# Channel attention and a highway layer on one core: held output stores, one chunk of v moved from DMA to TensorE, and a freer order of the t and x matmuls

## The chip, the core and the metric

The kernel runs on one core of a Trainium2 chip. The metric is the device time of one execution in microseconds (us). Five runs of the kernel before gave 279.01, 279.09, 278.99, 278.85 and 279.81, so the median is 279.01.

The core has a matrix engine (TensorE, PE in the profile, with its weight loads as PEld), a vector engine (VectorE, DVE), a scalar engine (ScalarE, ACT), GpSimd (POOL) and SyncE (SP). In this kernel POOL issues the loads and SP issues the stores and the DMA transposes. [...]

## The reference

There are four batches of q, k and v, each 6336 x 256 in f32. What is computed for each batch, cut to what matters:

```python
qn = q / (norm(q, axis=1) + 1e-6)            # norms over the 6336 rows
kn = k / (norm(k, axis=1) + 1e-6)
a = softmax(kn.T @ qn / tau)                 # 256 x 256, rows sum to 1
x = v @ a                                    # 6336 x 256
H = maximum(x @ w_h, 0)
T = 1 / (1 + exp(-(x @ w_t + b_t)))
out = T * H + (1 - T) * x
```

The attention is among the 256 channels, so all rows of q and k of a batch must have been read before the first output row of that batch.

## The kernel before

**Tiling.** A batch's rows are 48 steps of 128 rows, grouped into six chunks of eight steps, and a tail of 192 rows that counts as two steps. A chunk of q, k or v is one load of 1.05 MB that casts f32 to f16 on the way.

**Stage 1** (`stage1`, L381) takes a step of q and k and adds six matmuls into two PSUM banks, `sg0` and `sg1`: k'q, and k'k and q'q for the norms. There are 50 steps in a batch, 200 in all.

**The chain** (`plan_chain`, L409) follows the last step of a batch. It takes the diagonals from PSUM on DVE, powers on POOL, a broadcast matmul (`cqb`), scaling, exp, transposes (`eps`), the products of a with the two weights (`ah`), and leaves `mr`: 3 x 256 columns, which give x, h and t from v directly.

**Stage 2** (`plan_stage2`, L782) works on pairs of steps. There are 25 pairs in a batch, 100 in all, counted by g from 0 to 99. v is needed transposed. In batches 0 to 2, PE transposes it into PSUM (`transposes`, `vtps`) and ACT or DVE copies it out (`evac_vt`, `vtsb`). In batch 3, SP's DMA transposes it, a chunk at a time (`transpose_chunk`, L614, into `vT`). For each pair PE then makes h, t and x (4 matmuls each; x is accumulated onto `d`). ACT makes d from h (`relu`) and the gate from t. DVE makes `pp` and then `o`. Before t, its bank is filled with the bias: by a copy on ACT or DVE, or, from g = 66 on for every second pair, by a row matmul (`row0`, L673) into `sg1`, which stage 1 no longer needs.

**Order of the work.** The kernel is laid out by a planner, `Plan.run`, before anything is issued. It is a list scheduler: each task has an engine, a key, a length, things it waits for, and buffers it takes and gives back. An engine that is free takes the ready task with the lowest key. The order that comes out is the program's order. DMAs of POOL and SP are taken in order of their keys. `slot_of` (L355) spreads the steps of stage 1 of batches 1 to 3 between the pairs of stage 2: `ENDS` says at which pair stage 1 of a batch should end, `HEAD` how many steps come before the first pair.

**Buffers.** Nine chunks of q, nine of k, seven of v, three of the output `o`, four of `vT`, five of `vtsb`. A load waits for the buffer that it takes over. The rules that the change touches most are these:

```python
h = plan.add("PE", g, 0.435, 0.64, [ev] + ready[b] + ends_of[h_bank], ...)
t = plan.add("PE", g + 0.1, ..., [h] + b_ld + own + before + ends_of[t_bank], ...)
x = plan.add("PE", g + 0.2, 0.43, 0.63, [r, t], ...)
```

So t comes after h of its pair, and x after t and after relu. A store goes out as soon as its chunk is done (key g + 2). The identity and other constants are made first on POOL, then come the loads of batch 0: chunks 0 to 4, tail, chunk 5 in halves (both halves of q, then both of k).

## Time and profile before

| what | before |
|---|---|
| median of five runs | 279.01 us |
| the profiled execution's own time | 279.23 us |
| its span | 277.5 us |
| PE busy | 254.6 us (92%), 2610 matmuls |
| DVE, ACT, POOL busy | 181.4, 175.0, 54.5 us |
| loads (queue of POOL) | 39.20 MB written, 71.4% of 16 engines' span |
| stores and transposes (queue of SP) | 29.20 MB, 31.4% |
| HBM read and written | 78.38 and 25.95 MB |
| first and last start of PE's matmuls | 9.12 and near 271.6 us |

The span is the time from the first to the last instruction in the profile; the rest of an execution's time lies around it. Busy time of PE is a sum over matmuls that overlap, so it says where PE is at work, not how fast. The timeline gives the start of each instruction, its length, and in brackets how long the engine was idle before it and what ended that. A wait for several things is put down to the one that came last.

### The profile page before, as it was taken

The numbers are of one execution on the slowest core, as the hardware profiler recorded it, in microseconds if no ns is written. First come the engines' busy times: TensorE is split into PE (matmuls) and PEld (weight loads), VectorE is DVE, ScalarE is ACT, GpSimd is POOL, SyncE is SP. The second block draws the span as 40 slices with busy tenths as digits, with TensorE's granted clock in tenths as the row PEclk, the third lists the DMA queues.
The fourth block names the chain that finished last, engine by engine and source line by source line (L and its number), as shares of the span: only waits on it lengthen the run. The fifth ranks groups of instructions, "written<-read, shape, count | busy, mean of one in ns | idle before, by whom it ended". The sixth has DMA issues, their size and how long they took to land.

```text
span 277.5 us, 6499 instructions
## 1 busy us (share of the span) xinstructions
PE 254.6 (92%) x2610; PEld 228.0 (82%) x2610; DVE 181.4 (65%) x366; ACT 175.0 (63%) x328; POOL 54.5 (20%) x104
## 2 busy tenths in 40 slices
PE   0696879999999999999999999999999888999992
PEld 0595877899999898999999888999999767888881
DVE  1000035576766886777776886777777887898994
ACT  1000016666767776777767766777767779898982
POOL 7221445220212240211112421111111300000000
PEclk9998999999999999999999999999999999999997
DMA  6999999999999999999999999999999999999984
GB/s 110 210 215 213 210 207 212 216 213 288 257 246 282 287 212 288 240 272 279 244 262 287 257 243 280 220 296 264 242 284 289 234 261 171 355 222 313 251 307 180
DMA packets 29581, 68.80 MB, mean 248 GB/s; under 512 B 14832, under 2 KB 16496, under 8 KB 26608
## 3 DMA queue, kind: packets, MB, share of 16 engines
q0 software_dynamic: 12608, 39.20, 71.4%
q1 hardware_dynamic: 16944, 29.20, 31.4%
q8 instruction: 20, 0.33, 0.5%
q14 instruction: 9, 0.07, 0.1%
HBM read 78.38 MB, written 25.95 MB: 376 GB/s over the span
## 4 chain that ended last, share of the span: by engine, by line
PE 64%; DMA 30%; POOL 2%; DVE 2%; issue 1%; ACT 0%; DVEq 0%; POOLq 0%; ACTq 0%
PE t L642 12%; PE d L642 12%; PE h L642 12%; PE sg L393 10%; DMA v<-in_v_dram 10%; DMA k<-in_k_dram 8%; DMA vT<-v 7%; DMA q<-in_q_dram 6%; PE sg L394 5%; PE sg L395 5%; PE vtps L612 4%; PE t L673 1%; DVE pp L703 1%; POOL q L286 1%; PE ah L551 1%
## 5 line engine op out<-in xcount | busy, mean ns | idle before, releaser
L393 PE MATMUL sg<-q,k 128*128 128x256 f16 x384 | 96.0, 281 | 13.7 <-DMA k<-in_k_dram 13.7
L642 PEld LDWEIGHTS <-vtsb 128*128 128x128 f16 (+1 forms) x900 | 83.4, 99 | 9.8 <-issue 1.9
L394 PE MATMUL sg<-k 128*128 128x128 f16 x384 | 86.3, 225 | 0.0
L395 PE MATMUL sg<-q 128*128 128x128 f16 x384 | 85.6, 223 | 0.0
L703 DVE SCALAR_TENSOR_TENSOR pp<-uu,d 128x512 f32<-128x512 f32 (+1 forms) x100 | 68.3, 684 | 17.3 <-PE d L642 12.1
L696 ACT ACTIVATE uu<-t 128x512 f32<-128x512 f32 (+1 forms) x100 | 59.6, 597 | 27.4 <-PE t L642 25.4
L682 ACT ACTIVATE d<-h 128x512 f32<-128x512 f32 (+1 forms) x100 | 58.4, 584 | 22.3 <-PE h L642 22.0
L722 DVE SCALAR_TENSOR_TENSOR o<-h,pp 128x512 f32<-128x512 f32 x96 | 66.1, 689 | 2.9
L393 PEld LDWEIGHTS <-k 128*128 128x128 f16 x384 | 38.4, 100 | 16.1 <-DMA k<-in_k_dram 14.5
L405 ACT COPY t<-bias_all 128x512 f32<-128x512 f32 (+1 forms) x78 | 46.0, 589 | 1.9
L642 PE MATMUL d<-mr,vtsb 128*128 128x256 f16 x300 | 44.8, 272 | 0.1
L642 PE MATMUL t<-mr,vtsb 128*128 128x256 f16 x300 | 44.8, 272 | 0.1
L642 PE MATMUL h<-mr,vtsb 128*128 128x256 f16 x300 | 44.8, 272 | 0.0
L407 DVE COPY vtsb<-vtps 128x256 f32<-128x256 f32 (+1 forms) x62 | 26.1, 420 | 26.2 <-PE vtps L612 25.9
L395 PEld LDWEIGHTS <-q 128*128 128x128 f16 x384 | 38.6, 101 | 5.4
L394 PEld LDWEIGHTS <-k 128*128 128x128 f16 x384 | 38.6, 101 | 1.9
L642 PEld LDWEIGHTS <-vT 128*128 128x128 f16 x288 | 28.1, 98 | 5.7 <-DMA vT<-v 1.1
L612 PE MATMUL vtps<-ident,v 128*128 128x128 f32 x144 | 27.7, 274 | 1.8 <-ACT vtsb L405 1.1
L441 DVE SCALAR_TENSOR_TENSOR junk<-sg,ident 128x128 f32<-128x128 f32 x16 | 4.6, 287 | 37.3 <-PE sg L395 36.7
L484 ACT COPY gs<-sg 128x256 f32<-128x256 f32 x8 | 2.6, 376 | 38.2 <-DVE junk L441 38.2
L286 POOL DMA_DIRECT2D v<-in_v_dram x24 | 13.0, 543 | 48.7 <-PE d L642 9.5
L286 POOL DMA_DIRECT2D k<-in_k_dram x25 | 13.4, 538 | 39.9 <-DMA k<-in_k_dram 16.6
(66 smaller groups left out, 176.9 us busy)
## 6 DMA issues: line engine op xcount, KB each, us to landing
out_dram<-o SPq DMA_DIRECT2D x23, 1024.0 KB, 9.1
v<-in_v_dram POOLq DMA_DIRECT2D x24, 512.0 KB, 20.5
q<-in_q_dram POOLq DMA_DIRECT2D x23, 512.0 KB, 21.4
k<-in_k_dram POOLq DMA_DIRECT2D x23, 512.0 KB, 20.5
out_dram<-o SPq DMA_DIRECT2D x2, 512.0 KB, 2.6
out_dram<-ot SPq DMA_DIRECT2D x4, 192.0 KB, 6.6
q<-in_q_dram POOLq DMA_DIRECT2D x2, 256.0 KB, 14.7
k<-in_k_dram POOLq DMA_DIRECT2D x2, 256.0 KB, 12.0
```

What stands on the lines that cost most here:

```text
L286: nc.gpsimd.dma_start(out=t[:, s : s + n, :], in_=main_rows(src)[:, j * CH + s : j * CH + s + n, :])
L393: nc.tensor.matmul(sg[c][:, 0:C], kc, qa, start=first, stop=False)
L394: nc.tensor.matmul(sg[c][:, C : C + P], kc, kc, start=False, stop=False)
L395: nc.tensor.matmul(sg[c][:, C + P : C + 2 * P], qa[:, cs], qa[:, cs], start=False, stop=last)
L405: nc.scalar.copy(out=out, in_=in_)
L407: nc.vector.tensor_copy(out=out, in_=in_)
L612: nc.tensor.transpose(ps[:, u, 0:nr], words, ident0[0:nr, 0:nr])
L642: nc.tensor.matmul(out[0:nr, u, :], vt[u][kt][:, 0:nr], mr[kt][:, col * C : (col + 1) * C], **flags(u, kt))
L682: nc.scalar.activation(out=d[0:nr, :, :], in_=ps_t["h", b, i][0:nr, :, :], func=Act.Relu, scale=0.5)
L696: nc.scalar.activation(out=uu[0:nr, :, :], in_=ps_t.pop(("t", b, i))[0:nr, :, :], func=Act.Tanh, scale=-0.5)
L703: nc.vector.scalar_tensor_tensor(out=pp[0:nr, :, :], in0=el.pop(("uu", b, i))[0:nr, :, :], scalar=1.0, in1=ps_t.pop(("d", b, i))[0:nr, :, ...
L722: nc.vector.scalar_tensor_tensor(out=ot, in0=ps_t.pop(("h", b, i))[0:nr, :, :], scalar=0.0, in1=el.pop(("pp", b, i))[0:nr, :, :], op0=AluO ...
```

## The change

It has these parts.

1. **Held stores.** There are seven output buffers in place of three. `plan_holds` moves each chunk's store behind a small DMA on SP (`hold`, 1 KB) that reads the first row of the chunk four later, and so waits for the first result of that chunk. From pair 63 on nothing is held; the stores still held then go out together.
2. **Loads.** q, k and v have five buffers each. The constants come behind the first q and k on POOL (`serial`). Chunk 5 of batch 0 comes in quarters, q and k in turn, and stage 1 of batch 0 takes the tail before it. v of a chunk is loaded three pairs later in rank instead of two or ten earlier.
3. **First v chunk of batch 3.** It is transposed by PE, in f16, four transposes for a pair, and copied out by ACT or DVE; the other five chunks and the tail still go by DMA, planned 12 pairs ahead instead of 8, with three `vT` buffers instead of four.
4. **t and x.** t no longer waits for h. x waits for relu and only follows t on PE (`follows`: placed after t, without a wait for t's result in the plan).
5. **Keys.** `PRIO` gives each kind of task its own offset before and after pair 65; `ENDS` becomes 14.5, 35.5, 68; `HEAD` 7; nine `vtsb` buffers instead of five.

The code for sums of squares off PE (`APART`) is switched off, since `APART` is 0. The diff, cut:

```diff
-QK_BUFS = 9
-V_BUFS = 7
-AHEAD = 8
-MOVE = 100e3
-LOOK = 1.6
-POW = 1.0
-HEAD = 8
+QK_BUFS = 5
+V_BUFS = 5
+O_BUFS = 7
+LAG = 4
+UNTIL = 63
+AHEAD = 12
+BY_DMA = 1
+MOVE = 150e3
+APART = 0
+V_AHEAD = -3
+
+PRIO = {
+    "tr": (-1.66, -2.13), "ev": (-1.74, 0.56), "h": (1.61, 1.23), "bias": (1.7, -2.32),
+    "t": (2.04, 1.45), "relu": (-0.66, 0.47), "x": (1.97, 2.65), "gate": (-0.06, 5.26),
+    "prod": (0.43, -3.06), "res": (3.19, -3.22), "s1": (-0.71, 1.24), "sq": (-1.37, 0.36),
+}
+POW = 0.75
+HEAD = 7
-ENDS = [18, 42, 66]
+ENDS = [14.5, 35.5, 68]
...
-            x.n, x.left, x.at = n, len(x.deps), 0.0
+            x.n, x.left, x.at = n, len(x.deps) + len(x.follows), 0.0
...
                 free[e] = t + x.pitch
+                release(followers.get(x, ()), free[e])
...
-        "vT": 4, "vT_t": 1, "o": 3, "ot": 1, "uu": 3, "pp": 3, "vtsb": 5, "mr0": 2, "mr1": 2,
+        "sq": 2, "vT": 3, "vT_t": 1, "o": O_BUFS, "ot": 1, "uu": 3, "pp": 3, "vtsb": 9, "mr0": 2, "mr1": 2,
...
     consts = plan.add("POOL", len(plan.tasks), 0.6, 1.5, [], constants)
+    consts.serial = True
...
-    plan_load("q", 0, NJ - 1, 2)
-    plan_load("k", 0, NJ - 1, 2)
+    for part in range(4):
+        plan_load("q", 0, NJ - 1, 4, part)
+        plan_load("k", 0, NJ - 1, 4, part)
...
-                seq.append((NP * b + CH // 2 * j - (10 if b == B - 1 else 2), 1, "v", b, j))
+                seq.append((NP * b + CH // 2 * j - V_AHEAD, 1, "v", b, j))
...
+    def by_dma(b, j):
+
+        return natural(b) and j >= BY_DMA
+
+    def order_of(b):
+
+
+        if b:
+            return list(range(NS))
+        return [*range(S - CH), *range(S, NS), *range(S - CH, S)]
...
-            words = sub("v", b, 2 * i + u).bitcast(f32)
-            nc.tensor.transpose(ps[:, u, 0:nr], words, ident0[0:nr, 0:nr])
+            v = sub("v", b, 2 * i + u)
+            if natural(b):
+                for kt in range(2):
+                    nc.tensor.transpose(
+                        ps[:, u, :].bitcast(f16)[:, kt * P : kt * P + nr],
+                        v[:, bass.ts(kt, P)],
+                        ident[0:nr, 0:nr],
+                    )
+            else:
+                nc.tensor.transpose(ps[:, u, 0:nr], v.bitcast(f32), ident0[0:nr, 0:nr])
...
+        if natural(b):
+            copy(e, vt.bitcast(f16), ps.bitcast(f16))
...
+    begun, chunk_stores = {}, []
+
+    def hold(b, j):
+        nc.sync.dma_start(out=held_row, in_=og[(b, j)][0:1, 0, :])
+
+    def plan_holds():
+        for x, b, j in chunk_stores:
+            n = b * NJ + j + LAG
+            y, g = begun.get(n, (None, 1e9))
+            if g > UNTIL:
+                x.key = max(x.key, UNTIL + 1.6)
+                continue
+            x.key = g + 1.6
+            plan.add(
+                "SP", g + 1.5, 0.1, 0, [y], lambda n=n: hold(n // NJ, n % NJ), size=1024,
+            )
...
-                "PE", g + 0.1, 0.43 if own else 0.64, 0.63 if own else 0.84,
-                [h] + b_ld + own + before + ends_of[t_bank], lambda i=i: main_t(b, i),
+                "PE", pr("t", g), 0.43 if own else 0.64, 0.63 if own else 0.84,
+                b_ld + ready[b] + [ev] + own + before + ends_of[t_bank], lambda i=i: main_t(b, i),
...
-                "PE", g + 0.2, 0.43, 0.63, [r, t], lambda i=i: main_x(b, i),
+                "PE", pr("x", g), 0.43, 0.63, [r], lambda i=i: main_x(b, i), follows=[t],
```

In the program that the planner makes of it, stage 1 of batches 1, 2 and 3 ends when h of 12, 34 and 66 pairs has been issued on PE, against 19, 43 and 67 before. ACT has 352 instructions for 318, DVE 313 for 344. SP has 48 for 37: eleven more.

## The prediction

> **What bounds the kernel now.** I read the page's first two parts first.

> ```profile
> span 277.5 us, 6499 instructions
> PE 254.6 (92%) x2610; PEld 228.0 (82%) x2610; DVE 181.4 (65%) x366; ACT 175.0 (63%) x328; POOL 54.5 (20%) x104
> PE   0696879999999999999999999999999888999992
> DMA  6999999999999999999999999999999999999984
> ```

> PE and DMA are both full from 50 us on. Busy matmuls overlap, so I add PE up from start-to-start distances in the timeline: h, t or x of a pair 0.437 us, a stage-1 step 0.44, a transposed pair 0.22, a bias row 0.217, a batch's softmax 1.73. Over the order: 100 x 3 x 0.437 = 131.1; 200 x 0.44 = 88.0; 75 x 0.218 = 16.4; 20 x 0.217 = 4.3; 4 x 1.73 = 6.9; sum 246.7. The first matmul starts at 9.12, the last ends near 272.2, the span 5.3 later. In those 263.1 us, 16.4 are not work. The timeline of PE shows where:

> ```profile
> 24.94 0.28 PE L393 MATMUL sg<-q,k 128*128 128x256 f16 x1 [2.13 <-DMA k<-in_k_dram]
> 34.62 0.28 PE L393 MATMUL sg<-q,k 128*128 128x256 f16 x1 [0.78 <-DMA k<-in_k_dram]
> 40.76 0.28 PE L393 MATMUL sg<-q,k 128*128 128x256 f16 x1 [1.53 <-DMA k<-in_k_dram]
> 49.58 0.28 PE L393 MATMUL sg<-q,k 128*128 128x256 f16 x1 [0.20 <-DMA k<-in_k_dram]
> 219.92 0.38 PE L673 MATMUL t<-btb,row 128*128 128x512 f16 x1 [1.12 <-ACT gs L484]
> 226.19 0.44 PE L612 MATMUL vtps<-ident,v 128*128 128x128 f32 x2 [0.66 <-ACT vtsb L405]
> 227.09 0.44 PE L612 MATMUL vtps<-ident,v 128*128 128x128 f32 x2 [0.46 <-ACT vtsb L405]
> 235.92 0.61 PE L642 MATMUL h<-mr,vT 128*128 128x256 f16 x4 [0.81 <-DMA vT<-v]
> ...
> 26.00:28.00 2.00, 2.00 (x17) 0.50 1.02 205
> ```

> The bracket is PE's idle time and who ended it. A v load cost 0.58 more at 157.86. So waits are 8.3 in all, of which 3.83 come after the first h (which runs from 47.51 to 47.95). The last line, two-microsecond stretches, has the granted clock third from the end: 0.50. Half clock cost stage 1 of batch 0 about 5.2 (39.2 - 9.12 - 2.9 waits - 22 work). Some 2.4 are small losses after the first h.

> The timeline of SP shows what DMA transposes cost their queue:

> ```profile
> 217.69 13.43 SPq L620 DMA_TRANSPOSE vT<-v  x1
> 231.83 6.26 SPq L620 DMA_TRANSPOSE vT<-v  x1
> 244.41 3.07 SPq L620 DMA_TRANSPOSE vT<-v  x1
> ```

> The first landed after 18.2 us, at 235.9, as PE asked for it. From 217.7 to 262.6 SP does little else.

> [...] loads land 2.45 us apart (q 47.3, k 49.5, v 52.2), 1.05 MB in each: 428.

> **The change, part by part.**

> *Start.* q and k of chunk 0 pass the identity on POOL: issued at 0.74 instead of 1.42, so all loads land 0.68 earlier. The identity comes 1 us later; DVE first needs it near 36: 0. The last chunk of batch 0 comes in interleaved quarters behind the tail. Before, its first k half landed at 34.6, the rest near 35.8, and ten steps (4.4 us) ended at 39.1. Now the last quarter lands near 35.1 and two steps remain: 36.1, with 3 us gained. But in the order one step of batch 1 still stands ahead of the broadcast matmul; its k lands at 40.74 - 0.68 = 40.06. So the broadcast starts at 40.5 on full clock, not 41.66, and the first h could end near 46.9 instead of 47.95: -1.05. PE is idle for 4 us before it, though, longer than the 2.13 that led to half clock. At 0.85 for the step, 0.86 for the broadcast and 2 to 4 slow steps the first h ends near 48.2: +0.3. I take -0.35.

> *Loads.* Five q, k and v buffers for nine and seven; v comes after the q, k of like rank. From k at 48.9 loads land each 2.45: q2, k2 at 53.7, k3 58.6, v1 61.0, k4 65.9, v2 68.4, k5 73.3, v3 81.7. Adding up PE's order from a first h ending at 48.0, it asks for k2 at 55.0, k3 60.3, v1 62.5, k4 68.2, v2 69.9, k5 75.6, v3 83.8. The least cover is 1.3: free while loads keep that pace. Without stores ahead of about 95 us they should; if they slip 2 us, PE loses 0.7. Later stage 1 of batches 1 and 2 ends at 12 and 34 pairs instead of 19 and 43, batch 3 at 66 instead of 67. It is the same work in another place, on an engine without waits: 0. PE's sum is 247.6 after, 246.7 before.

> *Stores.* Each chunk's store stands behind a 1 KB DMA that reads the chunk four later, so it leaves some 3 chunks late; 7 output buffers cover it. Behind each hold on SP stand only stores, so no compute waits for it. At pair 62 the hold ends: five stores (5.2 MB) leave within about 8 us, near 210 to 218. Then come the transposes. DMA has room before, since loads wait for buffers.

> *Transposes.* Seven DMA transposes become six, and about 5 us of DMA time go. Four pairs of f16 go through PE: 4 x 0.22 = +0.9 on PE. Four copies of 512 f16: the nearest rows are 128x512 f32, 0.589 on ACT and 0.692 on DVE; bounds 0.3 and 0.7; I take 0.6, 2.4 us over two engines. Both ran at 9.3 in ten in 240 to 270, but with overlapping instructions. Between none and 1.2 of it reaches PE: I take 0.3. The first DMA transpose is now for pair 79. SP reaches it near 217, as before; pair 79 comes near 239. Even 18.2 us leaves 3 to 4. Chunks 4 and 5 wait for a vT buffer (three for four) until x of pairs 82 and 86, near 244 and 250; with 6.8 us they land at 251 and 257, asked for at 256 and 261.

> *Order of t and x.* x no longer waits for t in the plan but follows it on PE; t needn't follow h. In the middle PE has no gap to fill: 0. At the end of stage 1 of batch 3 the new order puts 3.1 us of ready work (with t of pair 68) ahead of the first bias row into the stage-1 bank, where 1.76 stood before: the 1.12 goes. Transposes are spread out with nine result buffers: 0.66 and 0.46 mostly go. The 0.81 goes with its transpose, the 0.20 and part of 0.58 too. After the first h I expect 1.0 of waits for 3.83: -2.8. If the softmax chain and copies keep ACT and DVE just as late elsewhere, this is zero.

> *Bias copies and vtsb.* ACT takes 48 vtsb copies for 13, DVE 31 for 62: 35 x 0.375 = 13 us more on ACT (175 in 277). ACT and DVE are busy 7 to 7.5 us in each ten before 217, so this hides beside PE: 0. Were they PE's pace there, it would cost up to 6.

> Sum: -0.35 - 2.8 + 0.9 + 0.3 = -1.95. The profiled execution had 279.23 for a span of 277.5; its span becomes 275.5. The median shown, 279.01, is 0.2 below that execution; minus 2.0 it is **277.0**.

> **The rivals.**

> *Full gain (0.17).* Clock stays up: -1.05; all 3.83 of waits go; +0.9: -4.0, 275.0. If the small losses shrink as well, 273.5. For it: the idle before 40.76 (1.5 us) left no slow stretch. Against it: four idle microseconds.

> *It cancels (0.16).* The end phase is held by ACT and DVE together. Their busy share of 9.3 in ten speaks for it, PE's own 1.42 us per pair (3 x 0.437 + half of 0.217) against it. The waits move but stay, -0.6, and the copies cost 1.2: -0.35 - 0.6 + 0.9 + 1.2 = +1.1 at worst, -0.5 at best: 278.5 to 279.5.

> *Slower by late transposes (0.10).* [...] In 60 to 210, 53.6 MB of loads were issued, 125 us at 428 GB/s; the other 25 us took 16.3 MB of stores, 650 GB/s. From pair 62 on 14 MB of stores (22 us; 33 at 428), six transposes near 5 (31) and 4.7 MB of v (11) ask for 64 to 75 us of DMA, where 65 are left. It decides when the first transpose lands more than 21 us after 217; every microsecond beyond costs one. With 25 to 27: +4 to +6 - 2: 281 to 283. Against it: loads are nearly out by then.

> *Slower by starved steps (0.09).* With five buffers a load starts only when its chunk is used up[...]. If loads fall to 2.6 us each, then 12 of them are 1.8 late, past the 1.3 of cover; 2 to 4 us are lost over 50 to 100: 279.3 to 281.

> **How the numbers follow.** Forecast as summed, 276 to 278.4: 0.48. With the rivals' 0.17, 0.16, 0.10 and 0.09 that is 1. About 0.2% (0.56 us) is what a measurement of this kernel can tell from no change. Faster: 0.48 + 0.17 and a sliver of the cancelling case, 0.67. Same: 0.14. Slower: 0.19. The range leaves out the best end of the full gain and the late transposes: 274.2 to 280.3; the forecast's own range is 275.8 to 278.3.

> **What would show it.** The first load at 0.74; stage 1 of batch 0 done near 36; a wait of about 4 us for k at 40.1 and a clock below 1.00 at 40 to 44; first h between 46.5 and 48. No PE wait for q, k or v over 0.3 between 50 and 210. No wait for gs at the first bias row of the end; PE's waits after 217 near 1. SP's first transpose near 217, vT never waited for. The prediction is wrong if PE waits on loads or vT for over 1 us, if a store holds up DVE's o, or if the stretch from 217 to the last matmul grows beyond 56 us (55.1 now; 52.4 of work then against 51.1).

## The result, and the profile after

The changed kernel takes 279.42 us (median of 36 executions) beside 279.32 for the kernel before (70 executions): a ratio of 0.9996, with a 95% interval of 0.9983 to 1.0009. No change can be told, where 277.0 was forecast. One thing did change: the kernel before lies between 278.85 and 280.45, the changed one between 277.35 and 282.19. Its eight fastest executions, up to 278.23, lie in the forecast's own range. Medians and ranges here are of all executions, a ratio is of those within 1.5% of the fastest of their kernel.

The profiled execution took 279.81, with a span of 278.0. These are the lines of its page that answer to those shown of before.

```profile
span 278.0 us, 6539 instructions
PE 255.5 (92%) x2626; PEld 229.2 (82%) x2626; DVE 167.4 (60%) x335; ACT 183.7 (66%) x363; POOL 56.4 (20%) x108
PE   0686959999999999999999999999999999999992
DMA  6999999999999999999999999999995999999995
```

PE's row has lost its three eights (215 to 236 us): the end phase is denser. In the sixth slice (35 to 42 us) there is a 5 where a 7 stood. DMA's row has a 5 near 210, and its last two slices are 9 and 5 instead of 8 and 4: DMA is idle in part before the end phase and busier in it. The timeline of PE has these waits (start, length, operation, and in brackets the idle time ahead of it and who ended it).

```profile
24.82 0.28 PE L431 MATMUL sg<-q,k 128*128 128x256 f16 x1 [2.21 <-DMA k<-in_k_dram]
41.59 0.28 PE L431 MATMUL sg<-q,k 128*128 128x256 f16 x1 [3.43 <-DMA k<-in_k_dram]
...
221.61 0.60 PE L777 MATMUL t<-mr,vtsb 128*128 128x256 f16 x4 [0.59 <-ACT t L515]
230.63 0.59 PE L668 MATMUL ah<-wht,et 128*128 128x512 f16 x2 [0.33 <-DVE o L857]
272.28 0.60 PE L777 MATMUL d<-mr,vT_t 128*96 128x256 f16 x4 [0.29 <-ACT d L817]
```

After the first h, which now starts at 49.77, only 1.48 us of waits are left (these three and 0.27 at 146.31): 1.0 was forecast, 3.83 stood before. The trouble is the second line. The first k of batch 1 lands at 41.59, not at 40.06, and PE has been idle for 3.43 us. What follows shows in the two-microsecond stretches of PE (length, busy time, count, granted clock, DMA share, GB/s):

```profile
26.00:28.00 2.00, 2.00 (x16) 0.50 1.00 198
...
42.00:44.00 2.00, 2.00 (x17) 0.69 1.10 218
44.00:46.00 2.00, 2.00 (x17) 0.50 1.04 209
46.00:48.00 2.00, 2.00 (x22) 0.96 1.09 219
```

The kernel before was at 1.00 in all three of the last stretches, as in this one:

```profile
42.00:44.00 2.00, 2.00 (x27) 1.00 1.03 207
```

The timeline of SP, after:

```profile
214.56 7.18 SPq L871 DMA_DIRECT2D out_dram<-o  x5
221.79 11.18 SPq L745 DMA_TRANSPOSE vT<-v  x1
...
233.69 7.56 SPq L745 DMA_TRANSPOSE vT<-v  x1
...
241.96 8.18 SPq L745 DMA_TRANSPOSE vT<-v  x1
```

Four of the five held stores have left by 217.7. The fifth waits for its chunk, whose last result DVE ends at 221.39, and the first transpose stands behind it: it is issued at 221.8 instead of near 217. It lands 17.2 us later, at 239.0; PE asks at 241.9.

**Where the time went.** At a marker in PE's order, the time less the work that stands ahead of it (by the same distances as in the prediction) is what PE has lost so far.

| marker | lost before | lost after | lost in between, after against before |
|---|---|---|---|
| last step of stage 1, batch 0 | 17.09 | 16.02 | -1.07 |
| last step of stage 1, batch 1 | 19.87 | 21.85 | +3.05 |
| last step of stage 1, batch 3 | 21.26 | 23.31 | +0.07 |
| last x of batch 3 | 25.33 | 25.11 | -2.27 |

With 0.88 more work for PE the sum is +0.66, which is what the last x shows (271.62 before, 272.28 after). The end phase gives about what was forecast: -2.27 and +0.88 are -1.4, where -2.8, +0.9 and +0.3 were summed. The start takes it.

### The profile page after: what moved, and what is told of

Read it like the earlier page. It is cut to its first block, busy times and chain, and to the rows that moved or that the text cites. A ratio compares the mean times of both kernels' runs of the same rounds, so it can differ in the third digit from the quotient of the medians.

```text
span 278.0 us, 6539 instructions
## 1 busy us (share of the span) xinstructions
PE 255.5 (92%) x2626; PEld 229.2 (82%) x2626; DVE 167.4 (60%) x335; ACT 183.7 (66%) x363; POOL 56.4 (20%) x108
## 4 chain that ended last, share of the span: by engine, by line
PE 81%; DMA 13%; issue 1%; ACT 1%; DVE 1%; POOL 1%; DVEq 0%; ACTq 0%; POOLq 0%
PE t L777 16%; PE h L777 15%; PE d L777 15%; DMA k<-in_k_dram 13%; PE sg L431 12%; PE sg L434 6%; PE sg L432 6%; PE vtps L737 6%; PE t L808 1%; PE ah L668 1%; PE cqb L609 1%; PE eps L658 1%; POOL q L310 1%; DVE pp L838 1%; ACT uu L831 0%
## 5 line engine op out<-in xcount | busy, mean ns | idle before, releaser
L838 DVE SCALAR_TENSOR_TENSOR pp<-uu,d 128x512 f32<-128x512 f32 (+1 forms) x100 | 68.4, 684 | 52.4 <-ACT uu L831 36.1
L777 PEld LDWEIGHTS <-vtsb 128*128 128x128 f16 (+1 forms) x948 | 89.2, 99 | 10.9 <-issue 1.6
L857 DVE SCALAR_TENSOR_TENSOR o<-h,pp 128x512 f32<-128x512 f32 x96 | 65.9, 688 | 2.4
L431 PEld LDWEIGHTS <-k 128*128 128x128 f16 x384 | 38.4, 100 | 17.3 <-DMA k<-in_k_dram 16.4
L777 PE MATMUL t<-mr,vtsb 128*128 128x256 f16 x316 | 47.4, 272 | 0.9 <-ACT t L515 0.9
L777 PE MATMUL d<-mr,vtsb 128*128 128x256 f16 x316 | 47.4, 273 | 0.0
L777 PE MATMUL h<-mr,vtsb 128*128 128x256 f16 x316 | 47.2, 272 | 0.0
L515 ACT COPY t<-bias_all 128x512 f32<-128x512 f32 x75 | 44.2, 589 | 2.0
L310 POOL DMA_DIRECT2D v<-in_v_dram x24 | 12.9, 537 | 74.2 <-PE vtps L737 41.6
L777 PEld LDWEIGHTS <-vT 128*128 128x128 f16 x240 | 23.5, 98 | 3.8
L310 POOL DMA_DIRECT2D q<-in_q_dram x27 | 14.5, 539 | 38.2 <-DMA q<-in_q_dram 9.9
L310 POOL DMA_DIRECT2D k<-in_k_dram x27 | 14.5, 538 | 31.9 <-DMA k<-in_k_dram 14.6
## 6 DMA issues: line engine op xcount, KB each, us to landing
q<-in_q_dram POOLq DMA_DIRECT2D x23, 512.0 KB, 17.2
```

Of the source, the lines that this page charges most:

```text
L310: nc.gpsimd.dma_start(out=t[:, s : s + n, :], in_=main_rows(src)[:, j * CH + s : j * CH + s + n, :])
L431: nc.tensor.matmul(sg[c][:, 0:C], kc, qa, start=first, stop=False)
L515: nc.scalar.copy(out=out, in_=in_)
L777: nc.tensor.matmul(out[0:nr, u, :], vt[u][kt][:, 0:nr], mr[kt][:, col * C : (col + 1) * C], **flags(u, kt))
L838: nc.vector.scalar_tensor_tensor(out=pp[0:nr, :, :], in0=el.pop(("uu", b, i))[0:nr, :, :], scalar=1.0, in1=ps_t.pop(("d", b, i))[0:nr, :, ...
L857: nc.vector.scalar_tensor_tensor(out=ot, in0=ps_t.pop(("h", b, i))[0:nr, :, :], scalar=0.0, in1=el.pop(("pp", b, i))[0:nr, :, :], op0=AluO ...
```

## The experiments

All comparisons are with the kernel before on the same chip at the same time; its medians were 279.22, 279.68, 279.11 and 279.10 in the four sets. A comparison across sets, such as with the 279.42 of the changed kernel, is that much less sure. Where nothing else is said, a kernel is the changed one with the edit shown.

### Set 1: the start, and the holds

**A filler for PE.** It keeps PE busy while it would wait for k of batch 1.

```diff
+    def fill():
+        ps = new("h", [P, 2 * C], f32, "fill")
+        for _ in range(34):
+            nc.tensor.matmul(ps[:, 0:P], ident, ident, start=True, stop=True)
...
         ready[b] = plan_chain(b, first, x, -50, [sums_of_q] if apart(b, 0) else [])
+        if b == 0:
+            y = plan.add("PE", -50.5, 0, 0, [x, consts], fill, take=["h"])
+            y.drop = [(y, "h")]
```

> The changed kernel with 34 matmuls of 128 columns (1.9 us of PE, their result is never read) put right behind the last stage-1 step of batch 0, where PE otherwise idles 3.4 us for k of batch 1; nothing else moves in any engine's order. Theory A (the idle start of batch 1 puts PE on half clock, and that takes back what the end gains): no clock below 0.9 between 42 and 48, first h near 48.3 instead of 49.8, time 1.5 us below the changed kernel, near 277.9. Rival B (the late load alone sets the first h, the clock is beside the point): first h at 49.8 or later, time the same within 0.3. Rival C (the loss lies in the end, with the held stores and the DMA): the same within 0.3.

Measured: 282.49 (278.17 to 287.40), ratio 1.0009 (0.9971 to 1.0047). The ratio is of the three faster executions alone, up to 281.21; the other three took 283.77 to 287.40. The profiled one is of these (287.22, span 285.5). In it the clock did what was expected, 1.00 from 24 us on, and the last step of stage 1 of batch 3 came at 216.77 instead of 218.44. Then the gain was lost several times over, as its timeline of PE shows:

```profile
242.10 0.61 PE L777 MATMUL t<-mr,vT 128*128 128x256 f16 x4 [1.45 <-DMA vT<-v]
252.90 1.03 PE L777 MATMUL t<-mr,vT 128*128 128x256 f16 x4 [4.96 <-DMA vT<-v]
```

The first DMA transpose landed 21.9 us after its issue, not 17.2, the second 19.8 after, not 12.3; the matmuls of the second line already took 1.03 us in place of 0.60. So there is a second matter: the transposes of the end are on an edge. By the medians none of the three times expected came.

**The last q and k chunk in halves again.**

```diff
-    for part in range(4):
-        plan_load("q", 0, NJ - 1, 4, part)
-        plan_load("k", 0, NJ - 1, 4, part)
+    plan_load("q", 0, NJ - 1, 2)
+    plan_load("k", 0, NJ - 1, 2)
```

> The changed kernel with the last q, k chunk of batch 0 loaded in halves as before, instead of quarters; the order of all other engines is the same. Theory A: k of batch 1 lands 0.6 to 0.8 earlier (near 40.9), stage 1 of batch 0 ends 0.8 later (38.8), so PE's idle time falls from 3.4 to about 2 and the clock stays up in most runs; first h near 48.2; time 1.2 to 1.6 below the changed kernel. Rival B (the late load alone): 0.7 below. Rival C: the same within 0.3.

Measured: 278.64 (277.45 to 279.01), ratio 0.9960 (0.9938 to 0.9981). The timeline of PE:

```profile
40.40 0.28 PE L430 MATMUL sg<-q,k 128*128 128x256 f16 x1 [2.43 <-DMA k<-in_k_dram]
```

k of batch 1 lands 1.2 us earlier than in the changed kernel. The clock still falls to 0.50 at 42 to 44, but is at 0.80 at 44 to 46, where the changed kernel had 0.50. Beside the changed kernel's median that is 0.8 us, what rival B had, and beside its ratio 1.0.

**The broadcast matmul ahead of the first step of batch 1.** The two change places on PE; nothing else moves.

```diff
-    for x in plan.run():
+    order = plan.run()
+    marks = [getattr(x, "mark", None) for x in order]
+    c = order.pop(marks.index(("cqb", 0)))
+    order.insert(marks.index(("s1", 1, 0)), c)
+    for x in order:
```

> The changed kernel with the softmax's broadcast matmul of batch 0 moved ahead of the first stage-1 step of batch 1 on PE; nothing else moves. Theory A: the broadcast starts near 40.6 instead of 42.05; PE's idle time is cut in two, but the clock may still fall, so between 0.7 and 2 us below the changed kernel. Rival B: the broadcast no longer waits for the load, so 1.4 below, with or without half clock. Rival C: the same within 0.3.

Measured: 279.29 (277.63 to 281.35), ratio 0.9998 (0.9963 to 1.0032). Behind the step, the broadcast had started at 42.05, only after k had come; ahead of it, it starts at 40.29. But PE has been idle 2.31 us by then and for 0.65 more until k comes; from 42 to 46 the clock falls. By its time alone this is rival C. The profile shows why so little came of it: getting past the wait was worth little with the clock at 0.54 and 0.61 behind it, and stage 1 of batch 3 ends only 0.45 earlier (217.99).

**No holds.** Each chunk's store is issued as soon as the chunk is done, and the small DMAs that hold are left out; PE, DVE, ACT and POOL keep their order.

```diff
+    order, early, gone = plan.run(), {}, set()
+    for z, b, j in chunk_stores:
+        early.setdefault(z.deps[0], []).append(z)
+        gone.add(z)
+    for x in order:
+        if x in gone or (x.size == 1024 and x.eng == "SP"):
+            continue
...
+        for z in early.get(x, ()):
+            z.fn()
```

> The changed kernel with every chunk's store issued as soon as its chunk is done, and no hold DMAs; all other engines keep their order. Theory A: the holds are neither gain nor loss, within 0.4 of the changed kernel; no new wait for loads over 0.5. Rival C (held stores crowd the DMA in the last 65 us): 1 us or more below the changed kernel, and the first vT lands earlier than 233. Rival D (holding lets the loads of 50 to 100 us arrive in time): PE waits for q, k or v by 1 to 4 us in all between 55 and 110, and the time is that much above.

Measured: 290.91 (289.13 to 291.64), ratio 1.0398 (1.0370 to 1.0425). SP now issues stores from 65.86 us on, and with five buffers for each of q, k and v PE waits for two loads of v, by 1.97 and 2.35. The timeline of PE:

```profile
88.72 0.44 PE L737 MATMUL vtps<-ident,v 128*128 128x128 f32 x2 [1.97 <-DMA v<-in_v_dram]
98.70 0.66 PE L737 MATMUL vtps<-ident,v 128*128 128x128 f32 x2 [2.35 <-DMA v<-in_v_dram]
```

The last step of stage 1 of batch 2 starts at 151.49 against 144.29, so 7.2 are lost by then: 0.9 before the first h (50.69 for 49.77), 4.3 in these two waits, and the clock is 0.52 in 100 to 102. From there to that of batch 3 both take 74.2; 3.5 more are lost up to the last x, 2.97 of them in waits for vT. Holding is worth about 11.5 us to this order by the medians, 10.7 at the last x: it pays for the small buffers.

### Set 2: do the transposes come late because they are issued late?

**Transposes planned 18 pairs ahead.** Only SP's order changes.

```diff
-AHEAD = 12
+AHEAD = 18
```

> The changed kernel with the DMA transposes planned 18 pairs ahead instead of 12. Only SP's order changes: the first transpose stands ahead of the last hold and the five stores that leave together, the others move up one place each; every other engine keeps its order. Theory L (the executions of the changed kernel differ because the first two transposes sometimes land after PE asks for them): the first transpose is issued near 206 instead of 221 and lands by 225, 15 us before PE needs it; the slow end of the executions goes: median 278.5 to 279.0, none above 280. Rival S (they differ by what the clock does in the first 50 us): no change, median 279.4, from 277.4 to above 281.

Measured: 284.73, with one execution at 278.22 and five between 282.90 and 286.65; with one left to compare there is no ratio. Theory L falls: the transposes leave earlier, and five of six executions are slower than any of the changed kernel. SP's timeline in the profiled execution (span 283.9):

```profile
208.26 3.66 SPq L745 DMA_TRANSPOSE vT<-v  x1
...
219.80 21.03 SPq L745 DMA_TRANSPOSE vT<-v  x1
...
276.14 0.43 SPq L869 DMA_DIRECT2D out_dram<-ot  x1
```

The first transpose went through in 3.66. The second kept the queue for 21.03, landed after 26.3, and the two loads of v issued beside it from 222.20 on took 18.8 and 21.5 us in place of the 11.2 that one took near there in the changed kernel. PE hardly waited (0.43 for vT), but all stores behind that transpose were late: the span ends 7.8 us after the last store's issue, in the changed kernel 3.2 (274.84 to 278.0). So an early issue does not help, and what runs beside a transpose is the next suspect. How far it can go shows in the DMA between 230 and 240 us; first the changed kernel, where PE did not wait for vT:

```profile
DMA packets 2729, 2.58 MB, mean 258 GB/s; under 512 B 2391, under 2 KB 2391, under 8 KB 2584
```

and the kernel with the filler, where it did:

```profile
DMA packets 2217, 1.25 MB, mean 125 GB/s; under 512 B 2076, under 2 KB 2076, under 8 KB 2181
```

Loads of v and transposes (mostly packets under 512 B) ran side by side in both, and the DMA time of the two queues was 1.13 and 1.14 times the stretch (64.4 + 48.8 and 51.2 + 62.6%); the bytes were half.

**All three edits together:** filler, halves, and 18 pairs ahead.

> The three edits together: the last q and k chunk of batch 0 in halves, 34 matmuls of the identity with itself behind stage 1 of batch 0 (their product is never read), the transposes planned 18 pairs ahead. Theory L with the start term: full clock from 30 us on gives 1.7 us back, the halves 0.4 to 0.7 (k of batch 1 lands near 40.4), no wait for vT: 276.8 to 277.4 with a spread below 1.5 us. Rival S: planning the transposes earlier adds nothing, and executions above 280 stay as with the filler alone.

Measured: 284.12 (278.16 to 293.40), ratio 0.9998 (0.9977 to 1.0019) for its nine fastest of 22. In the profiled execution (286.96) stage 1 of batch 3 ended at 216.0, 2.4 us earlier than in the changed kernel, and a wait of 3.99 for vT at 255.50 and late stores gave it away. Neither theory had the spread right.

**The changed kernel once more.**

> The changed kernel itself once more, beside these on the same chip. Both theories: median 279.0 to 279.8, lowest near 277.5, highest above 281. If its profiled execution is one of the slow ones, theory L wants a wait for vT between 240 and 255 in it, Rival S only a clock below 0.8 before 50.

Measured: 280.02 (278.64 to 282.56), ratio 1.0019 (1.0001 to 1.0037). Its profiled execution (280.52) has no wait for vT; k of batch 1 comes at 41.49 after 3.52 of idling, and the clock is 0.58 and 0.57 in 42 to 46.

**The old order of t and x, 18 pairs ahead.**

```diff
-        ... b_ld + ready[b] + [ev] + own + before + ends_of[t_bank], lambda ...
+        ... [h] + b_ld + ready[b] + [ev] + own + before + ends_of[t_bank], lambda ...
...
-        ... [r], lambda i=i: main_x(b, i), follows=[t],
+        ... [r, t], lambda i=i: main_x(b, i),
```

> As the kernel with the transposes 18 pairs ahead, but in the plan t again waits for h and x for t, as before the change; the plan comes out anew for PE, DVE and ACT. Theory O (the waits after 217 went away because t and x may be placed freely): 1.5 to 2.5 us slower than that kernel, with waits for gs, vtsb or o of 2 us or more after 217. Rival P (the keys, the nine result buffers and the chunk on PE did it): within 0.5 us of it.

Measured: 283.52 (280.95 to 285.25), ratio 1.0124 (1.0076 to 1.0171). Since DMA ends this one too (7.6 us from its last store's issue to the end of the span), and the kernel that it was to be compared with came out at 284.73, it says nothing on O or P. It was done again in set 4.

### Set 3: loads and transposes kept apart

**Eight v buffers for five.** By the plan, the last v loads leave ahead of the transposes.

```diff
-V_BUFS = 5
+V_BUFS = 8
```

> The changed kernel with eight v buffers for five; q and k keep five. Every engine keeps its order, but the last four v loads no longer wait for buffers that PE or a DMA transpose gives back: they leave near 185 to 213 instead of 210 to 240, into the stretch where the DMA engines are idle in part, and none runs beside a transpose. Theory C (a v load and a DMA transpose that run together slow each other; that is why vT comes late in some executions): each transpose is issued in under 8 us, the first lands within 13 us, and the spread goes: median 278.0 to 278.6, none above 279.5. Rival D (the five stores that leave together at 214 hold up the transposes): as the changed kernel, 279.0 to 280.0 with some above 281.

Measured: 279.50 (277.33 to 281.08), ratio 1.0004 (0.9985 to 1.0022). The timeline of POOL has the last v chunk's load, and SP's the transposes:

```profile
208.02 0.53 POOL L310 DMA_DIRECT2D v<-in_v_dram  x1 [8.23 <-PE vtps L737]
```

```profile
219.65 14.14 SPq L745 DMA_TRANSPOSE vT<-v  x1
...
234.50 5.28 SPq L745 DMA_TRANSPOSE vT<-v  x1
...
240.50 4.78 SPq L745 DMA_TRANSPOSE vT<-v  x1
...
247.18 1.75 SPq L745 DMA_TRANSPOSE vT<-v  x1
```

In the changed kernel the last load of v left at 239.57. The first transpose, behind five stores, is no faster (it lands after 17.5, so the 13 expected were wrong). The others take 5.28, 4.78 and 1.75 instead of 7.56, 8.18 and 2.45. The median did not fall as theory C had it. But what is left follows the clock: the ten executions with a mean granted clock of 0.992 or more took 277.33 to 279.28, the eight with 0.982 took 280.05 to 281.08, the four between them 279.21 to 280.28. So with loads and transposes apart the clock makes the difference. That it is the clock of the start, no profile of a slower execution shows here; the kernels with the filler below speak for it.

**Holding ended one chunk earlier.**

```diff
-UNTIL = 63
+UNTIL = 60
```

> The changed kernel with holding ended one chunk earlier: four of the five stores leave near 205 instead of 214, the fifth when its chunk is done; only one hold is gone from SP's order. Rival D: the transposes meet fewer stores, the first lands by 233, the spread shrinks: median 278.2 to 278.8, none above 280. Theory C: the loads of v still run beside the transposes: median 279.0 to 280.0, the slow executions stay.

Measured: 279.27 (277.33 to 282.60), ratio 1.0003 (0.9980 to 1.0026). Executions above 281 stay; by its times Rival D falls. In the profiled one (281.35) the first transpose, with one store close ahead of it, took 7.52 and landed at 231.98, 7 us earlier than in the changed kernel; but then two v loads left together at 232.54, and the transpose beside them took 13.87.

**Filler, halves and eight v buffers.**

> The start repaired (last chunk of batch 0 in halves, 34 matmuls of the identity with itself behind stage 1 of batch 0, whose product is never read) and eight v buffers. Theory C with the start term: stage 1 of batch 3 ends near 216.0 as with the start repaired before, and no wait for vT follows: 276.3 to 277.3, spread below 1.5 us. Rival D: executions from 278 to above 284, as with the filler alone.

Measured: 277.18 (277.05 to 277.35), ratio 0.9932 (0.9918 to 0.9945). This is faster than the kernel before, 2.2 us below the changed kernel's median, and the spread of its five executions is 0.3 us. PE's timeline:

```profile
37.56 2.06 PE L913 MATMUL fill<-ident 128*128 128x128 f16 x34
40.28 0.28 PE L430 MATMUL sg<-q,k 128*128 128x256 f16 x1 [0.67 <-DMA k<-in_k_dram]
...
218.87 0.60 PE L776 MATMUL t<-mr,vtsb 128*128 128x256 f16 x4 [0.59 <-ACT t L514]
...
269.54 0.60 PE L776 MATMUL d<-mr,vT_t 128*96 128x256 f16 x4 [0.29 <-ACT d L816]
```

The clock is 1.00 in every stretch from 24 to 60. The last x starts at 269.54, 2.74 earlier than in the changed kernel, with the same end phase: 53.84 from the last step of stage 1 to it, there too.

### Set 4: what carries it, and what each part of the change is worth

**Filler and eight v buffers, quarters kept.**

> As the kernel with halves, filler and eight v buffers (277.18), but with the quarters of the change in place of the halves. Theory S (half clock in the first 50 us is what differs between executions once loads and transposes are apart): full clock from 30 us on, the quarters cost 0.4 to 0.9: 277.5 to 278.1, spread below 1 us. Rival H (k of batch 1 by halves carries it, the filler adds nothing): as with eight v buffers alone, 277.3 to above 280, median near 279.3.

Measured: 277.87 (277.39 to 278.52), ratio 0.9947 (0.9927 to 0.9968). Against eight v buffers alone (277.33 to 281.08) the filler is the only difference, and it carries the steadiness; the halves are worth the other 0.7, across sets. The pair of this kernel and the one with the filler alone differ in the number of v buffers only: 277.87 against 282.49.

**The old order of t and x,** with filler, halves and eight v buffers.

> Halves, filler and eight v buffers as in the kernel of 277.18, but in the plan t waits for h again and x for t; the plan comes out anew for PE, DVE and ACT. Theory O (the free order took the waits after 217 away): waits for gs, t and o come back, 278.5 to 279.5. Rival P (keys, result buffers and the chunk on PE took them away): within 0.5 us of 277.2.

Measured: 279.47 (279.20 to 279.62), ratio 1.0006 (0.9996 to 1.0016). The old order costs 2.3 us here: theory O by size. Its waits are only in part where theory O had them. This one came back, ahead of the end phase's pairs:

```profile
219.95 0.60 PE L776 MATMUL h<-mr,vtsb 128*128 128x256 f16 x4 [0.90 <-ACT gs L600]
```

From the last step of stage 1 to the last x it takes 55.63 in place of 53.84, for the same work, while the waits of 0.2 or more sum up to 1.23 and 1.22. The 1.8 are stops too short for the timeline to call them waits: start-to-start distances between 217 and 236 that are 0.10 to 0.25 too long, one after another. Another 0.66 is a wait for v at 123.28, which does not belong to the end. The keys stayed those of the free order; how the old order does with keys of its own, and the free order with the old keys, was not run.

**The first v chunk of batch 3 by DMA as before,** with filler, halves and eight v buffers.

```diff
-BY_DMA = 1
+BY_DMA = 0
```

> Halves, filler and eight v buffers, but the first v chunk of batch 3 is transposed by DMA as before the change: four times 0.22 us less on PE, four copies less. Theory W (PE's own work sets the end here): 0.9 us less work, and PE waits for the first vT, which lands 16 to 18 us after its issue near 212 to 219, for up to 3 us: 276.2 to 279. Rival G (DMA sets the end): a sixth transpose takes 4 to 6 us of DMA time, the last store is later: 279 to 282.

Measured: 279.07 (278.47 to 279.68), ratio 0.9993 (0.9981 to 1.0006). PE's timeline:

```profile
239.31 0.61 PE L776 MATMUL t<-mr,vT 128*128 128x256 f16 x4 [1.41 <-DMA vT<-v]
```

PE has 0.88 less work and its last x starts 1.54 later. The chunk on PE gains 1.9. The wait at 239.31 is 1.41 of it. The first transpose, now issued at 204.18, kept SP for 13.92, so the hold and the five stores behind it left at 218 in place of 211, and every later transpose with them.

**Quarters and early tail alone,** on the kernel before.

> The kernel before with two parts of the change alone: chunk 5 of batch 0 in quarters, q and k in turn, and the tail's steps ahead of it. Its buffers, stores, keys and transposes stay; the plan comes out anew. Theory S: stage 1 of batch 0 ends some 1 us earlier, k of batch 1 lands 0.5 to 0.8 later than 40.76 and PE's wait for it grows past 2.5 us, half clock follows: 279.5 to 281. Rival Q (an earlier end of stage 1 is worth what the prediction said): 278.0 to 278.8.

Measured: 280.12 (279.93 to 280.89), ratio 1.0032 (1.0019 to 1.0044). PE's timeline:

```profile
41.09 0.39 PE L399 MATMUL sg<-q,k 128*128 128x256 f16 x1 [3.48 <-DMA k<-in_k_dram]
```

Stage 1 of batch 0 ends 1.6 us earlier, PE waits 3.48 instead of 1.53, and the clock is 0.73, 0.50 and 0.91 from 40 to 46. Theory S as expected: this part of the change is a loss by itself, of 1.0 us in the medians.

## Why the prediction was wrong

The forecast was a sum of four terms: start -0.35, waits after the first h -2.8, transposes on PE +0.9, copies +0.3.

**The start failed.** The table of losses has +1.98 for it (-1.07 and +3.05), 2.3 worse than the term. The step that failed is "its k lands at 40.74 - 0.68 = 40.06". It landed at 41.59, for two reasons.

- "All loads land 0.68 earlier" was wrong. The timeline of POOL:

```profile
1.23 0.66 POOL L310 DMA_DIRECT2D q<-in_q_dram  x1 [0.79 <-POOLq L1052]
```

  The load does not take the memset's place at 0.74: it leaves at 1.23, and the bracket puts the 0.79 ahead of it down to POOL's own sequencer. The first matmul moved from 9.12 to 9.06, so 0.6 of the 0.68 was not there. In the kernel before with quarters, whose loads still stand behind the identity, it is at 8.94.
- The quarters were taken to cost nothing to what is loaded behind them. From the first matmul to k of batch 1 it takes 31.6 in the kernel before; the mean is 31.4 in five kernels with halves (31.03 to 31.66) and 32.3 in ten with quarters (31.86 to 32.68). That is 0.9. From 28 to 34 us, while the quarters come in, the DMA engines of the changed kernel are busier (1.21 to 1.24, 1.12 to 1.15 before) and move less (199 to 202 GB/s, 200 to 213 before). Which part of it costs is open: with the pieces, the order of q and k changed, and q of batch 1 is issued at 31.82 instead of 27.52 with halves.

The 3 us expected from an earlier end of stage 1 of batch 0 did not come either: it ended at 38.0, not 36.1, since the last quarter landed at 35.88, not 35.1, and PE, without a break since 24.8, still had almost five steps then, not two. With k later than that, it cost nothing.

The price of the half clock was right for the changed kernel: from -1.05 to +0.3 is 1.35. From k's arrival to the end of stage 1 of batch 3 the runs have:

| kernel | PE idle before k | clock in 42 to 46 | k arrives | until stage 1 of batch 3 ends |
|---|---|---|---|---|
| changed | 3.43 | 0.69, 0.50 | 41.59 | 176.85 |
| changed, again | 3.52 | 0.58, 0.57 | 41.49 | 176.85 |
| halves | 2.43 | 0.50, 0.80 | 40.40 | 176.85 |
| holding ended earlier | 3.15 | 0.50, 0.50 | 40.95 | 178.05 |
| 18 pairs ahead | 3.79 | 0.50, 0.50 | 41.41 | 177.72 |
| eight v buffers | 2.62 | 1.00, 1.00 | 40.64 | 175.65 |
| filler | 1.81 | 1.00, 1.00 | 41.29 | 175.48 |
| filler, eight v buffers | 1.50 | 1.00, 1.00 | 41.20 | 175.67 |
| filler, halves, eight v buffers | 0.67 | 1.00, 1.00 | 40.28 | 175.42 |

Full clock gives 175.4 to 175.7. One stretch of half clock (3.41 us in the trace's record of the granted clock; the first three rows) gives 1.2 to 1.4 more, two stretches in a row (6.83 us; the next two) 2.0 to 2.6 more. The prediction named the four idle microseconds and then weighed full and half clock against each other at -0.35; it should have summed the half clock and left the full one to a rival: in the table, half clock followed every wait of 3.15 us or more. With k 1.5 late and half clock in full (0.65 more than weighed) the term is +1.8, near the +1.98 measured.

**The waits after the first h were right by their sum.** 1.48 for 1.0 forecast and 3.83 before; with the short stops, the end phase lost 2.27 less than before, where -2.8 and +0.3 were summed. That the free order matters is shown by the old order put back (2.3 slower, 1.8 of it in the end phase). But it does not show the way that the prediction had: there the waits of 0.2 or more are no longer than in the free order (1.23 and 1.22), and the 1.8 lie in stops too short to be listed. What took away the listed waits of the kernel before is not shown one by one; the keys and the nine result buffers stayed in that run.

**The chunk on PE** was booked at +1.2 for work and copies, with 0.81 taken off by its vanished wait. Put back on DMA in the repaired kernel it is 1.9 worse. The work was sized rightly (0.88), and its four copies took 2.0 us (two of 0.586 on ACT, two of 0.420 on DVE) where 2.4 were taken. That the transpose it replaces keeps SP and the stores behind it for 13.92 us, and lets the next vT come 1.41 late, was not in the sum.

**The holds at nothing, and the loads on time,** were right for the change as a whole: PE waits for no q, k or v from 50 to 210. It is a trade within the change, though, not a free part: without the holds 11.5 us are lost.

**The late transposes** were a rival with 0.10: "it decides when the first transpose lands more than 21 us after 217". In the changed kernel it landed 22.0 after 217, and PE, which asked at 241.9, did not wait; so that line was drawn too early. In the kernel with the filler it landed 25 after 217, and PE waited 1.45 for it and 4.96 for the second. The place was right. That the filler's median, 282.49, lies in the 281 to 283 given is luck, with six executions from 278.17 to 287.40. The cause was only half right: the stores ahead do slow the first transpose (it landed 7 us earlier where holding ended earlier), but there the median and the slow executions stayed. What matters more are the v loads that five buffers and the later rank of v put beside the transposes. The part on loads ("free while loads keep that pace") looked at 50 to 100 us only, where it holds. What shows this is the filler's pair: with five v buffers 278.17 to 287.40, with eight 277.39 to 278.52. For the changed kernel itself it stays an inference: seven of its 36 executions, and three of 22 in the second set, were above 281, as one of 22 with eight v buffers was; no profile fell on one of them. The nearest is that of holding ended earlier (281.35 for 279.81): its last x comes 1.2 us later, 1.2 by a second stretch of half clock, 0.65 in the end phase, less the 0.64 by which k came earlier. Also open is why a start that is 1.7 us earlier makes the transposes so much later; the order on SP and POOL is the same.

## What to carry to other kernels

When work is taken from ahead of a load that has to be waited for anyway, the wait grows, and PE may come out of it at half clock, as here (3.43 us of idling for 1.53, and a clock of 0.50 for 1.00 at 44 to 46): price the next arrival first, then the clock behind the longer wait, and only then the work that was saved. Buffers cut to what one stretch needs move the loads of a later stretch (here the last load of v, at 239.57 with five buffers and at 208.02 with eight); look there for what they will run beside, here transposes by DMA. And give a kernel that runs just in time more than one execution: here its median and its best execution were 2 us apart (279.42 and 277.35), and the best one shows what a repair may be worth.

## What the runs showed of the hardware

```profile
40.64 0.28 PE L431 MATMUL sg<-q,k 128*128 128x256 f16 x1 [2.62 <-DMA k<-in_k_dram]
```

  The wait near 24.5 was 1.67 to 2.35 us in the seventeen profiles; in eight the clock then fell to 0.50 (waits of 1.92 to 2.35), in nine it stayed at 1.00 (1.67 to 2.12). An estimate from the 1.92 and the 1.89: a wait of 3.4 us escapes only where a boundary lies within 0.2 us of its middle.
- **DMA transposes were slower with cast loads beside them.** The second or third transpose of a v chunk kept SP's queue for 4.8 to 5.6 us with no load beside it (eight v buffers), 7.3 to 12.5 with one beside it for most of that time, and 13.9 to 21.0 with two that left together. In two profiles one that was issued just before two such loads kept the queue for only 4.7 and 5.8, but landed 15.5 and 15.6 after its issue. The first behind five stores took 10.8 to 14.1 with five v buffers or eight.
- **Four quarters instead of two halves of a cast load of q and of k delayed the loads behind them:** from the first matmul to k of the next batch it took 32.3 us in place of 31.4. The order of q and k changed with them.
- **The filler fitted into PE's wait.** It has 34 matmuls, 2.06 us, where PE had idled for 3.43; 1.81, 1.50 and 0.67 us of wait were left in the three kernels of the table. The clock is 1.00 from 40 to 48 us in all six profiles with it.
